# Pooled attention feeding a feed-forward network: the q tiles of batches 1 to 7 transposed by VectorE in 32 by 32 blocks

## The chip, the cores and the metric

The kernel runs on one core of one Trainium2 chip. The metric is the device time of one execution in microseconds (us); less is better. The inputs lie in HBM, and the output is written there.

## The reference

The input is q, k and v of 8 batches, 8 heads, 576 positions and 64 dimensions, and two weight matrices of 512 x 2048 and 2048 x 512, all float32. Cut to what matters:

```python
k_p = k.reshape(B, H, Sp, 8, D).mean(axis=3)      # 576 positions pooled to 72
v_p = v.reshape(B, H, Sp, 8, D).mean(axis=3)
scores = (1 / sqrt(D)) * q @ k_p.transpose(0, 1, 3, 2)
scores = scores - max(scores, axis=-1)
attn = exp(scores)
attn = attn / (sum(attn, axis=-1) + 1e-9)
attn_out = attn @ v_p                             # (8, 8, 576, 64)
x = attn_out.transpose(0, 2, 1, 3).reshape(4608, 512)
h = x @ w_in
return maximum(0.01 * h, h) @ w_out               # (4608, 512)
```

## The kernel before

**The feed-forward part** is most of the work. The 4608 rows of x are taken in nine pieces of 512 (c = 0 to 8), and the 2048 hidden columns in sixteen strips of 128 (f). Each matrix is held as a rounded high part and the remainder, and each product is made of three matmuls (high by high, low by high, high by low). `m1` (L661 to L663) makes a strip of h in PSUM (`ph`), ScalarE applies the leaky step to it (L666) and rounds it to `gh` (L669), and VectorE takes the remainder `gl` (L670). `m2` (L685 to L687) multiplies that with w_out into four accumulators (`acc`), which `store` copies out (L707 and L708) and sends to HBM. The runs are: c = 0 with the first eight strips, c = 1 with all, c = 0 with the rest (the first half comes back from HBM as `partial`), then c = 2 to 8.

**The weights** arrive as bits (`w_bits`, L161 and L165) and are split on the chip into the high and low parts by `convert`: four ScalarE and VectorE operations in `head` (L183 to L189), two in `tail` (L193 and L194). This goes on during the first 160 us, beside the attention of batches 0 and 1.

**The attention** of a batch is split into units, by tiles of 128 or 64 positions; each batch has four tiles of 128 and one of 64, named q1_0 to q1_4 for batch 1. `load_q` fetches a tile with one DMA, positions on the partitions, all 8 heads by 64 dimensions in a row of 512. `q_unit` (L364) has TensorE transpose it in four blocks of 128 columns into a PSUM bank, `pq` (L368), and ScalarE copies that to `qT` (L370), which then holds two heads by 64 dimensions on the partitions. `s_unit` multiplies qT with the pooled keys (`pss`, L393), VectorE takes the maximum of each row (`red`, L401) and ScalarE the exponentials (`e`, L403). `norm_unit` divides by the sum (L414 and L415 on VectorE, `at` on GpSimd, L417 and L421). `p_unit` transposes the result on TensorE (`pp`, L442) and splits it (`pT_hi`, `pT_lo`, `pT_rem`, L444 to L452). `av_unit` multiplies with the pooled values (`pa`, L467 to L470) and writes x, split in two parts (L484 and L485), transposed as `m1` needs it.

**Buffers.** q tiles of batch 0 lie in places that x takes later; those of all other batches share two buffers (`two`, tag `q`), and their qT share two others. The `pq` bank comes from `bank`; for batches 1 to 7 that is one of two PSUM banks, which `pss`, `pp`, `pa`, `pk` and `pv` use too.

**What sets the order.** TensorE's order is written out by hand: the string FIRST for batch 0, and behind it the loop over `beats`, which puts attention units between the matmuls of `m1` and `m2`; `line_up` arranges the units. `qu` asks for the tile two further on as soon as a tile's `q_unit` is issued. The order on the other engines is found by a scheduler that looks at dependences and estimated times. Nearly all DMAs are issued by SyncE (SP), in one queue, in order. Its DMAs take eight completion counters in turn, and each waits for the DMA that is eight before it.

Of the kernel before, what the change touches and what calls it, by code (L numbers as in the profile page):

```python
# [10 lines left out]
F32 = mybir.dt.float32  # L11
# [13 lines left out]
def tile_pooled_attention_ffn(  # L25
# [9 lines left out]
    nc = tc.nc  # L35

    P = 128
# [6 lines left out]
    NK = DM // P  # L44
# [31 lines left out]
    two = ctx.enter_context(tc.tile_pool(name="two", bufs=2))  # L76
# [30 lines left out]
    for g in range(2):  # L107
        r = slice(32 * g, 32 * g + 32)
# [97 lines left out]
    def bank(b, name):  # L206
        nonlocal turn
        pool, tag = banks[turn % len(banks)] if b == 0 else banks[0]
        turn += 1
        return pool.tile([P, NK, P], F32, tag=tag, name=name)  # L210
# [104 lines left out]
    def load_q(b, t):  # L315
        s0, n = tiles[b][t]
        if b == 0:
            qr = one.tile([P, H, D], F32, tag=f"xh1_{t}" if t < NK else "xl1_0", name=f"q{b}_{t}")
        else:
            qr = two.tile([P, H, D], F32, tag="q", name=f"q{b}_{t}")  # L320
        nc.sync.dma_start(qr[:n], q[b, :, s0 : s0 + n, :].rearrange("h s d -> s h d"))
        return qr

    def place_k(b, sums, rem):
# [38 lines left out]

    def q_unit(b, t, qr):  # L364
        n = tiles[b][t][1]
        pq = bank(b, f"pq{b}_{t}")
        for p in range(NK):
            nc.tensor.transpose(pq[:, p, :n], qr[:n, 2 * p : 2 * p + 2, :], ident[:n, :n])  # L368
        qT = two.tile([P, NK, P], F32, tag="qT", name=f"qT{b}_{t}")
        nc.scalar.copy(qT[:, :, :n], pq[:, :, :n])  # L370
        return qT
# [142 lines left out]
    def attention(b):  # L514
# [5 lines left out]
        def loads():  # L520
            (start_k, st["k"]), (start_v, st["v"]) = load_k(b), load_v(b)
            start_k()
            q_of[b, 0] = load_q(b, 0)
            q_of[b, 1] = load_q(b, 1)
            start_v()
            for t in range(2, 5):
                q_of[b, t] = load_q(b, t)
# [18 lines left out]
        def qu(t):  # L546
            def f():
                st["qT", t] = q_unit(b, t, q_of[b, t])
                after = every.index((b, t)) + 2
                if after < len(every) and every[after] not in q_of:  # L550
                    q_of[every[after]] = load_q(*every[after])
            return f
# [210 lines left out]
    for b in range(2, B):  # L763
        for j, piece in enumerate(PIECES[b]):
            c = 2 + (2 * TAIL + S * (b - 2) + piece[0][0]) // CH
# [85 lines left out]
```

## Time and profile before

| what | value |
|---|---|
| three runs | 1004.41, 1009.0 and 1011.04 us; median 1009.0 |
| profiled execution, its own time | 1006.54 us |
| its span in the profile | 1004.8 us |
| mean granted TensorE clock | 0.982 |
| HBM read and written | 46.14 MB and 10.49 MB |
| DMA packets under 512 B | 39856 of 65006 |

PE is TensorE, DVE VectorE, ACT ScalarE, POOL GpSimd and SP SyncE. A row of the timeline gives the start in us, the duration in us, the engine, the line of the code, the operation with output and inputs, and in brackets the idle time before it and what ended it. "x4" in a row means four instructions in one. In the rows that group a whole stretch, the numbers behind the bar are busy us, mean ns of one, and idle us before them with what ended it. Matmuls are pipelined, so the durations of neighbours overlap; their starts tell the pace. The profiled execution is the one whose rows are used for durations.

### The profile page before, as it was taken

How to read it: one execution, taken by the hardware profiler on the slowest of the kernel's cores; microseconds unless marked ns; L12 is line 12 of the kernel's file. 1: busy time of each engine (PE TensorE's matmuls, PEld its weight loads, DVE VectorE, ACT ScalarE, POOL GpSimd, SP SyncE). 2: the span in 40 equal slices, each digit the busy share in tenths (PEclk: the TensorE clock that was granted, in tenths of full speed). 3: DMA queues.
4: the chain of work that ended last, by engine and by line, in shares of the span. 5: the costliest groups of instructions: out<-in, count | busy, mean ns of one | idle time of the engine just before them, and what ended most of it. 6: DMA issues, size and time to landing. Idle time of an engine off the chain costs nothing.

```text
span 1004.8 us, 12738 instructions
## 1 busy us (share of the span) xinstructions
PE 952.5 (95%) x4536; PEld 778.1 (77%) x4536; DVE 371.5 (37%) x902; ACT 428.2 (43%) x1386; POOL 177.4 (18%) x292
## 2 busy tenths in 40 slices
PE   4468899999999999999999999999999999999998
PEld 3457678888787778888887888788877888788886
DVE  5998639323432322233232333233223322221111
ACT  4677766234433343434343434344443433322221
POOL 3602200401116610132013301220110100100000
PEclk9689999999999999999999999999999999999999
DMA  9955311312033400121022202110100010001001
GB/s 241 267 171 149 88 60 42 103 34 69 1 104 101 105 11 17 58 74 32 6 64 58 58 1 69 46 29 1 58 22 11 1 48 1 1 1 42 0 1 42
DMA packets 65006, 57.44 MB, mean 57 GB/s; under 512 B 39856, under 2 KB 48048, under 8 KB 64944
## 3 DMA queue, kind: packets, MB, share of 16 engines
q1 hardware_dynamic: 64944, 56.64, 19.8%
q8 instruction: 36, 0.59, 0.3%
q14 instruction: 26, 0.21, 0.1%
HBM read 46.14 MB, written 10.49 MB: 56 GB/s over the span
## 4 chain that ended last, share of the span: by engine, by line
PE 88%; DVE 5%; ACT 4%; issue 1%; DMA 1%; SPq 1%; POOL 0%; DVEq 0%; ACTq 0%; POOLq 0%
PE ph L661 13%; PE acc L685 13%; PE ph L663 13%; PE ph L662 13%; PE acc L687 13%; PE acc L686 13%; PE pss L393 4%; PE pp L442 3%; PE pq L368 1%; ACT e L403 1%; PE pa L468 1%; PE pa L467 1%; PE pa L470 1%; PE pa L469 1%; SPq L240 1%
## 5 line engine op out<-in xcount | busy, mean ns | idle before, releaser
L661 PE MATMUL ph<-xh,w 128*128 128x512 f32 x576 | 235.8, 409 | 0.0
L685 PE MATMUL acc<-w,gh 128*128 128x512 f32 x576 | 233.7, 406 | 0.0
L663 PE MATMUL ph<-xh,w 128*128 128x512 f32 x576 | 226.3, 393 | 0.0
L662 PE MATMUL ph<-xl,w 128*128 128x512 f32 x576 | 226.1, 393 | 0.0
L687 PE MATMUL acc<-w,gl 128*128 128x512 f32 x576 | 225.7, 392 | 0.0
L686 PE MATMUL acc<-w,gh 128*128 128x512 f32 x576 | 225.5, 392 | 0.0
L670 DVE TENSOR_TENSOR gl<-ph,gh 128x512 fp32r<-128x512 f32 x144 | 99.4, 690 | 263.2 <-ACT gh L669 262.3
L666 ACT ACTIVATE ph<-ph 128x512 f32<-128x512 f32 x144 | 84.2, 585 | 250.4 <-PE ph L663 250.3
L403 ACT ACTIVATE e<-pss,red 128x72 f32<-128x72 f32 (+1 forms) x320 | 98.2, 320 | 115.5 <-DVE red L401 115.3
L417 POOL TENSOR_TENSOR at<-e,red 128x256 f32<-128x256 f32 (+1 forms) x76 | 47.4, 624 | 543.7 <-DVE red L415 267.8
L663 PEld LDWEIGHTS ph<-xh,w 128*128 128x128 f32 x576 | 108.7, 189 | 24.0
L687 PEld LDWEIGHTS acc<-w,gl 128*128 128x128 f32 x576 | 108.4, 188 | 23.8
L685 PEld LDWEIGHTS acc<-w,gh 128*128 128x128 f32 x576 | 108.5, 188 | 22.3 <-issue 1.6
L661 PEld LDWEIGHTS ph<-xh,w 128*128 128x128 f32 x576 | 108.8, 189 | 21.9 <-issue 1.4
L686 PEld LDWEIGHTS acc<-w,gh 128*128 128x128 f32 x576 | 108.7, 189 | 19.7
L662 PEld LDWEIGHTS ph<-xl,w 128*128 128x128 f32 x576 | 108.9, 189 | 19.1
L669 ACT CAST gh<-ph 128x512 fp32r<-128x512 f32 x144 | 85.4, 593 | 3.1
L401 DVE TENSOR_REDUCE red<-pss 128x4 f32<-128x288 f32 (+1 forms) x80 | 36.1, 453 | 94.3 <-PE pss L393 93.2
L403 ACT ACTIVATION_READ_ACCUMULATOR e<-pss,red 128x1 f32 (+1 forms) x320 | 65.4, 204 | 0.0
L393 PEld LDWEIGHTS pss<-kT,qT 128*128 128x128 f32 (+1 forms) x320 | 47.1, 183 | 14.4 <-ACT qT L370 4.9
L393 PE MATMUL pss<-kT,qT 128*128 128x144 f32 (+1 forms) x320 | 53.8, 295 | 4.1 <-ACT qT L370 4.1
L448 DVE TENSOR_TENSOR pT_lo<-pp,pT_hi 128x256 fp32r<-128x256 f32 (+1 forms) x80 | 31.7, 396 | 66.0 <-ACT pT_rem L445 65.3
(93 smaller groups left out, 844.1 us busy)
## 6 DMA issues: line engine op xcount, KB each, us to landing
out_dram<-o SPq DMA_DIRECT2D x35, 256.0 KB, 2.9
q<-in_q_dram SPq DMA_DIRECT2D x32, 256.0 KB, 3.9
w_bits<-in_moe_w_in_dram SPq DMA_DIRECT2D x16, 512.0 KB, 3.7
w_bits<-in_moe_w_out_dram SPq DMA_DIRECT2D x16, 512.0 KB, 3.5
k0raw<-in_k_dram SPq DMA_DIRECT2D x16, 256.0 KB, 3.7
k1raw<-in_k_dram SPq DMA_DIRECT2D x16, 256.0 KB, 4.4
v0raw<-in_v_dram SPq DMA_DIRECT2D x16, 256.0 KB, 3.8
v1raw<-in_v_dram SPq DMA_DIRECT2D x16, 256.0 KB, 5.6
```

What stands on the lines that cost most here:

```text
L393: nc.tensor.matmul(sc[:n, 2 * SP * i : 2 * SP * (i + 1)], qT[:, p, :n], kT[:, p, :, :].rearrange("d i s -> d (i s)"), start=True, stop=True,)
L403: ins = nc.scalar.activation(e[:n, h, :], scv[:n, h, :], AF.Exp, bias=mx[:n, h : h + 1], accum_out=sm[:n, h : h + 1],)
L417: eng.tensor_tensor(at[:n, 0:2, :].rearrange("a i (h s) -> a (i h) s", h=2), e[:n, :, 0:MAIN], sm[:n].unsqueeze(2).broadcast_to([n, 4, MAI ...
L661: nc.tensor.matmul(ph, w[:, 0, ks], xh[kk], start=kk == 0, stop=False)
L662: nc.tensor.matmul(ph, w[:, 0, ks], xl[kk], start=False, stop=False)
L663: nc.tensor.matmul(ph, w[:, 1, ks], xh[kk], start=False, stop=kk == NK - 1)
L666: nc.scalar.activation(ph, ph, AF.Prelu, alpha=0.01)
L669: casts.append(nc.scalar.copy(gh, ph))
L670: nc.vector.tensor_tensor(gl, ph, gh.bitcast(F32), op=ALU.subtract)
L685: nc.tensor.matmul(a, gh[:, r], hi, start=first, stop=False)
L686: nc.tensor.matmul(a, gh[:, r], lo, start=False, stop=False)
L687: nc.tensor.matmul(a, gl[:, r], hi, start=False, stop=last)
```

## The change

For batch 0 nothing changes. For the others a q tile is no longer loaded by one DMA with positions on the partitions. Its 512 columns are four pairs of heads (p) by two heads of a pair (i) by two halves of 32 dimensions (c); its positions are blocks (g) of 32. Sixteen DMAs, one for each i, c and p, put the blocks into the partitions that their columns will have after the transpose: block row 2i + c holds the 32 columns c of head i. Each DMA writes 32 partitions, and moves runs of 32 numbers (128 bytes) where the one DMA moved runs of 64 (256 bytes). VectorE then transposes every block of 32 by 32 in its place, with one instruction for the tile, from the q buffer into qT. The four transposes on TensorE, the PSUM bank and ScalarE's copy of these tiles go: 28 tiles of 128 positions and 7 of 64.

```diff
@@ load_q
-        nc.sync.dma_start(qr[:n], q[b, :, s0 : s0 + n, :].rearrange("h s d -> s h d"))
+        if b == 0:
+            nc.sync.dma_start(qr[:n], q[b, :, s0 : s0 + n, :].rearrange("h s d -> s h d"))
+            return qr
+
+        blocks = qr.rearrange("a h d -> a (h d)").rearrange("a (p g d) -> a p g d", p=NK, d=32)
+        src = q[b, :, s0 : s0 + n, :].rearrange("(p i) (g s) (c d) -> i c s p g d", i=2, s=32, c=2)
+        for i in range(2):
+            for c in range(2):
+                r = 32 * (2 * i + c)
+                for p in range(NK):
+                    nc.sync.dma_start(blocks[r : r + 32, p, : n // 32, :], src[i, c, :, p])
         return qr
@@ q_unit
         n = tiles[b][t][1]
+        if b > 0:
+
+            qT = two.tile([P, NK, P], F32, tag="qT", name=f"qT{b}_{t}")
+            blocks = qr.rearrange("a h d -> a (h d)").rearrange("a (p s) -> a p s", p=NK)
+            nc.vector.transpose(qT[:, :, :n], blocks[:, :, :n])
+            return qT
```

In the changed kernel the lines behind the first insertion are 10 further down, and those behind the second 16: the new DMA is L331, the new transpose L380, L401 becomes L417, and L661 becomes L677.

The order moves at three places. The first is SP's queue about 34 us from the start, where the first two tiles of batch 1 are loaded between strips of weights (`w0_bits4` is strip 4 of w_in, `w1_bits4` of w_out). Before:

```order
L161 DMA w0_bits3_182<-in_moe_w_in_dram 128x4x256
L165 DMA w1_bits3_184<-in_moe_w_out_dram 128x1024
L321 DMA q1_0_365<-in_q_dram 128x8x64
L321 DMA q1_1_566<-in_q_dram 128x8x64
L161 DMA w0_bits4_461<-in_moe_w_in_dram 128x4x256
L165 DMA w1_bits4_463<-in_moe_w_out_dram 128x1024
L161 DMA w0_bits15_1631<-in_moe_w_in_dram 128x4x256
L161 DMA w0_bits5_555<-in_moe_w_in_dram 128x4x256
```

And now:

```order
L161 DMA w0_bits3_182<-in_moe_w_in_dram 128x4x256
L165 DMA w1_bits3_184<-in_moe_w_out_dram 128x1024
L331 DMA q1_0_365<-in_q_dram 32x4x32 x16
L161 DMA w0_bits4_476<-in_moe_w_in_dram 128x4x256
L165 DMA w1_bits4_478<-in_moe_w_out_dram 128x1024
L331 DMA q1_1_581<-in_q_dram 32x4x32 x14
L161 DMA w0_bits5_570<-in_moe_w_in_dram 128x4x256
L331 DMA q1_1_581<-in_q_dram 32x4x32 x2
L161 DMA w0_bits15_1711<-in_moe_w_in_dram 128x4x256
```

Two issues have become 32, and strip 4 and one DMA of strip 5 stand between the pieces of q1_1 and the rest. Further on, q1_4, q2_0 and q2_1 follow each other in SP's queue with one or two weight DMAs between them, sixteen pieces each.

The second place is DVE's list at about 53 us, in the conversion of strip 2 (`w0_t2`, `w1_t2`) and the last score unit of batch 0 (`red0_4`). Before:

```order
L189 ISA w0_t2_519<-w0_bits2_178,w0_t2_519 128x1024
L485 TENSOR_TENSOR xl0_3_409<-pa0_1_3_546,xh0_3_405 128x256
L186 SCALAR_TENSOR_TENSOR w1_t2_569<-w1_bits2_180,w1_t2_569 128x512
L401 TENSOR_REDUCE red0_4_0_581<-pss0_4_0_577 64x4
L401 TENSOR_REDUCE red0_4_1_591<-pss0_4_1_587 64x4
L194 TENSOR_TENSOR w0_2_518<-w0_t2_519,w0_2_518 128x512
L189 ISA w1_t2_569<-w1_bits2_180,w1_t2_569 128x1024
L414 TENSOR_SCALAR red0_4_0_581<-red0_4_0_581 64x4
```

And now:

```order
L189 ISA w0_t2_534<-w0_bits2_178,w0_t2_534 128x1024
L380 STREAM_TRANSPOSE qT1_0_771<-q1_0_365 128x512
L501 TENSOR_TENSOR xl0_3_424<-pa0_1_3_561,xh0_3_420 128x256
L186 SCALAR_TENSOR_TENSOR w1_t2_599<-w1_bits2_180,w1_t2_599 128x512
L417 TENSOR_REDUCE red0_4_0_611<-pss0_4_0_607 64x4
L417 TENSOR_REDUCE red0_4_1_621<-pss0_4_1_617 64x4
L380 STREAM_TRANSPOSE qT1_1_838<-q1_1_581 128x512
L194 TENSOR_TENSOR w0_2_533<-w0_t2_534,w0_2_533 128x512
L189 ISA w1_t2_599<-w1_bits2_180,w1_t2_599 128x1024
L430 TENSOR_SCALAR red0_4_0_611<-red0_4_0_611 64x4
```

The transposes of q1_0 and q1_1 stand among work that was there before; L194, L189 and the normalisation of batch 0's last tile come behind the second of them. Later transposes stand behind the maximum of the second score unit of the tile two before, which frees the qT buffer: q1_2 behind `red1_0_1`, q1_4 behind `red1_2_1`, q2_1 behind `red1_4_1`.

The third place is TensorE's list in the steady part, at about 228 us, around the first tile of batch 2. Before:

```order
L685 MATMUL acc1_3_1534<-w1_14_1761,gh1_14_2022 128x512
L686 MATMUL acc1_3_1534<-w1_14_1761,gh1_14_2022 128x512
L687 MATMUL acc1_3_1534<-w1_14_1761,gl1_14_2023 128x512
L368 MATMUL pq2_0_2129<-ident_87,q2_0_1100 128x128 x4
L661 MATMUL ph0_9_2138<-xh0_0_402,w0_9_1386 128x512
L662 MATMUL ph0_9_2138<-xl0_0_406,w0_9_1386 128x512
L663 MATMUL ph0_9_2138<-xh0_0_402,w0_9_1386 128x512
```

And now:

```order
L701 MATMUL acc1_3_1614<-w1_14_1841,gh1_14_2102 128x512
L702 MATMUL acc1_3_1614<-w1_14_1841,gh1_14_2102 128x512
L703 MATMUL acc1_3_1614<-w1_14_1841,gl1_14_2103 128x512
L677 MATMUL ph0_9_2228<-xh0_0_417,w0_9_1466 128x512
L678 MATMUL ph0_9_2228<-xl0_0_421,w0_9_1466 128x512
L679 MATMUL ph0_9_2228<-xh0_0_417,w0_9_1466 128x512
```

The four transposes are gone, and the rest of TensorE's list is as it was.

## The prediction

> **What bounds the kernel now.** I read the busy shares and the chain of waits first, then the busy time by stage.
>
> ```profile
> span 1004.8 us, 12738 instructions
> PE 952.5 (95%) x4536; PEld 778.1 (77%) x4536; DVE 371.5 (37%) x902; ACT 428.2 (43%) x1386; POOL 177.4 (18%) x292
> PE 88%; DVE 5%; ACT 4%; issue 1%; DMA 1%; SPq 1%; POOL 0%; DVEq 0%; ACTq 0%; POOLq 0%
> ...
> 0.00:58.00 58.00, 27.82 (x134) 22.98 (x134) 45.75 (x115) 34.45 (x136) 25.33 (x42) 0.79 0.93 249
> 58.00:75.00 17.00, 12.21 (x52) 9.44 (x53) 15.57 (x36) 15.03 (x32) 1.48 (x2) 0.80 0.48 152
> 75.00:150.00 75.00, 67.27 (x332) 53.90 (x331) 46.46 (x115) 51.67 (x169) 11.37 (x20) 0.98 0.33 100
> 150.00:900.00 750.00, 745.14 (x3580) 609.11 (x3579) 247.85 (x612) 303.50 (x1008) 139.24 (x228) 1.00 0.15 41
> ```
>
> The stage rows give, after the stretch, the busy us of PE, weight load, DVE, ACT and POOL, then the granted clock, the DMA share and GB/s. From 150 us on PE works 745.14 of 750 us: what leaves PE's list there shortens the run by its own length. Up to 75 us DVE and ACT are the full ones (15.57 and 15.03 of 17 us), and PE waits for them. So the change must be costed twice: as PE time after 150 us, and as DVE and SP work before.
>
> **PE, after 150 us: the gain.** Each removed tile is four transposes between matmuls that run back to back. One tile of 128 rows and one of 64:
>
> ```profile
> 227.43 0.40 PE L686 MATMUL acc<-w,gh 128*128 128x512 f32 x1
> 227.66 0.39 PE L687 MATMUL acc<-w,gl 128*128 128x512 f32 x1
> 227.89 0.60 PE L368 MATMUL pq<-ident,q 128*128 128x128 f32 x4
> 228.24 0.48 PE L661 MATMUL ph<-xh,w 128*128 128x512 f32 x1
> 228.56 0.40 PE L662 MATMUL ph<-xl,w 128*128 128x512 f32 x1
> ...
> 289.14 0.39 PE L663 MATMUL ph<-xh,w 128*128 128x512 f32 x1
> 289.46 0.46 PE L368 MATMUL pq<-ident,q 64*128 64x64 f32 x4
> 289.85 0.50 PE L685 MATMUL acc<-w,gh 128*128 128x512 f32 x1
> 290.18 0.39 PE L686 MATMUL acc<-w,gh 128*128 128x512 f32 x1
> ...
> L368 PE MATMUL pq<-ident,q 128*128 128x128 f32 x96 | 14.4, 272 | 0.0
> L368 PE MATMUL pq<-ident,q 64*128 64x64 f32 x24 | 2.7, 235 | 0.0
> ```
>
> Starts count here, since the durations overlap. A plain step is 227.66 − 227.43 = 0.23 us. From L687 at 227.66 to the second matmul behind the transposes (228.56) it is 0.90 us, where two steps would take 0.46: the tile costs 0.44. The small one costs 290.18 − 289.14 − 0.46 = 0.58. The last two rows, of the stretch from 150 us on, count 96/4 = 24 large and 24/4 = 6 small tiles: 24 × 0.44 + 6 × 0.58 = **14.0 us** gone. The score matmuls behind read qT, which DVE now makes about a tile earlier; with a third of DVE busy there (247.85 of 750) and ACT rid of a copy, nothing new should end last in this stage. Without that cover (qT late by a DVE operation) it would be up to 30 × 0.7 = 21 us.
>
> **PE, before 150 us.** Five q1 tiles go, 4 × 0.44 + 0.58 = 2.3 us. Part of that time PE waits for others anyway, so I count 1 us (bounds 0 and 2.3).
>
> **DVE: the transposes.** The trace of before holds none. Nearest are one-pass DVE rows of the same 128x512 shape, and the ACT copy that goes:
>
> ```profile
> L185 DVE TENSOR_SCALAR w_t<-w_bits 128x512 int32<-128x512 int32 x32 | 13.9, 439 | 1.6 <-DMA partial<-o 1.3 <-ACT w_bits L183 0.2
> L194 DVE TENSOR_TENSOR w<-w_t,w 128x512 fp32r<-128x512 f32 x32 | 24.1, 763 | 2.6 <-ACT w L193 2.5
> L370 ACT COPY qT<-pq 128x512 f32<-128x512 f32 x32 | 19.1, 595 | 27.8 <-PE pq L368 27.7
> ```
>
> So between 0.44 and 0.76 us; I take 0.6, the middle, as no row says which is nearer. Two of them (q1_0, q1_1) stand where DVE is full, near 54 us: **+1.2** (0.9 to 1.5). The others stand where DVE is about 60% busy (46.46 of 75) or less, and cost nothing unless their data is late. [...]
>
> **SP: sixteen issues for one.** This is the term that can eat the gain. What SP spends on an issue:
>
> ```profile
> L321 SPq DMA_DIRECT2D q<-in_q_dram x33: 367/390/616, 74.2 to 817.2; - x33
> DMA to landing us min/median/max: 2.9/3.8/3.9
> ...
> L240 SPq DMA_DIRECT2D k0raw<-in_k_dram x16: 596/602/737, 0.7 to 559.4; - x16
> L165 SPq DMA_DIRECT2D w_bits<-in_moe_w_out_dram x16: 327/341/547, 16.0 to 164.9; - x16
> ```
>
> An issue over 128 partitions takes 0.34 to 0.39 us (L165, L321), one over 64 takes 0.60 (L240, and the 0.616 of L321 is a tile of 64 rows). Fewer partitions are dearer, and 32 are in no row. I take t = 0.65 us a piece: the nearest row and 0.05 between issues. Below, eight completion counters in turn and about 3.6 us to landing allow no less than 3.6/8 = 0.45; above, as much again as from 128 to 64 gives 0.85 and the same ratio 1.0.
>
> In the steady stage 16 × 0.65 = 10.4 us a tile fall into 850/30 = 28 us. The start is where they matter, since DVE works in order and now stands still until all sixteen pieces of a tile have landed:
>
> ```profile
> L321 SPq DMA_DIRECT2D q<-in_q_dram x2: 368/1994/3620, 34.3 to 35.4; - x2
> DMA to landing us min/median/max: 8.7/8.7/8.7
> q<-in_q_dram SPq DMA_DIRECT2D x32, 256.0 KB, 3.9
> ...
> 54.43 0.80 DVE L401 TENSOR_REDUCE red<-pss 64x4 f32<-64x288 f32 x2
> 55.16 0.67 DVE L194 TENSOR_TENSOR w<-w_t,w 128x512 fp32r<-128x512 f32 x1
> 55.76 0.67 DVE L189 CUSTOM_DVE_ANT_0 w_t<-w_bits,w_t 128x1024 uint16<-128x1024 uint16 x1
> 56.55 0.17 DVE L415 RECIPROCAL red<-red 64x4 f32<-64x4 f32 x1
> 57.44 0.41 DVE L414 TENSOR_SCALAR red<-red 64x4 f32<-64x4 f32 x1 [0.72 <-ACT e L403]
> ...
> 56.86 0.61 POOL L417 TENSOR_TENSOR at<-e,red 64x256 f32<-64x256 f32 x1 [13.10 <-DVE red L415]
> 57.52 0.67 PE L442 MATMUL pp<-ident,at 64*128 64x64 f32 x3 [2.85 <-POOL at L417]
> ```
>
> The transpose of q1_1 comes behind the two maxima at 54.43, so at 55.2 + 0.6 (q1_0's) = 55.8. Its pieces: before, q1_1 was issued at 35.4 and landed 8.7 us later, at 44.1, the last of two tiles of q (2 × 256 KB, 2.1 us at the 249 GB/s of that stage), so all that was older had landed at 42. The eighth piece of q1_0 can go then, at the latest. Behind it SP has eight pieces of q1_0, the pair of w4 (0.9), fourteen pieces of q1_1, one weight DMA (0.4), and two pieces: 42 + 24t + 1.3 + 3.6 to land = 62.5 at t = 0.65. DVE stands from 55.8 to 62.5, less the 0.7 us that it idled there anyway: X = 24t − 9.6 = **6 us** (1.2 at t = 0.45, 14.4 at 1.0). Behind the waiting transpose are L194, L189 and the reciprocal L415; POOL's at (13.10 idle) and PE's pp (2.85 idle) wait for that one, so the stall reaches PE in full. [...]
>
> What is late next: from about 82 us, when the transpose of q1_2 (behind the max at 81.00) frees its buffer, SP has the pieces of q1_4, q2_0 and q2_1, 48 issues nearly in a row.
>
> ```profile
> 81.00 0.44 DVE L401 TENSOR_REDUCE red<-pss 128x4 f32<-128x288 f32 x1
> 106.37 0.46 DVE L401 TENSOR_REDUCE red<-pss 128x4 f32<-128x288 f32 x1 [1.54 <-PE pss L393]
> 121.92 0.45 DVE L401 TENSOR_REDUCE red<-pss 64x4 f32<-64x288 f32 x1 [0.32 <-POOL at L421]
> 123.71 0.37 PE pp L442 x3
> ```
>
> q2_1 is transposed behind the max at 121.92 (122.9 with one transpose more ahead), and its buffer comes free at 107.3, behind the max at 106.37. It is in time while 107.3 + 16t + 3.6 < 122.9, t < 0.75; with the queue, Y = 82 + 48t + 1.7 + 3.6 − 122.9 = 48t − 35.6 beyond that. PE's pp at 123.71 follows at once, so Y would reach the end too. At 0.65 it is nothing.
>
> **The sum:** −14.0 − 1 + 1.2 + 6 = −7.8 us. On the profiled execution, whose span is 1004.8 and whose time 1006.5, that is 998.7. The three runs shown have a median of 1009.0, 2.5 above it; the four times together average 1007.8, so I forecast **1000.0**, a gain of 0.8%. One per cent is about what a measurement of this kernel can tell from no change.
>
> **The rivals.** (a) Small pieces are issued fast, t about 0.45: X is 1, and the time 1007.8 − 14.0 − 1 + 1.2 + 1 = 995. For it: a piece moves 16 KB where the L240 row moves 128; against it: the 64-row q tile, half the bytes of the large one, has the longer issue. [...]
>
> (b) Slower: an issue over 32 partitions continues the trend, t = 1.0. Then X = 14.4 and Y = 12.4, and the time is 1007.8 − 13.8 + 26.8 = 1021. The place is SP's queue alone; it takes the whole gain back from t = 0.82 (X + Y = 13.8) and is slower by 1% from about 0.95. For it: 0.34 to 0.60 for half the partitions; against it: 64 partitions take 0.60 whatever they move, which looks like a flat price.
>
> (c) No gain to speak of: t near 0.8, or transposes that also come late at the boundaries between runs, a few us in sum: 1007.8 − 13.8 + 9 + 4 = 1007. For it: the 48 issues leave q2_1 only 1.6 us of slack; against it: 28 us per tile later on.
>
> **How the numbers follow.** Forecast 0.42 (own range 996 to 1004), (a) 0.30 (991 to 998), (c) 0.15 (1004 to 1013), (b) 0.13 (1013 to 1045). Faster by over 1% (under 997.7) is nearly all of (a) and a quarter of the forecast, 0.28 + 0.11 = 0.39; slower by over 1% (above 1017.9) most of (b) and an odd stall, 0.13; the rest, 0.48, within 1%. The range 990 to 1014 leaves out most of (b) and little else.
>
> **What would show it.** The 96 + 24 pq rows behind 150 us are gone, and PE stays full from there to the end, in a stage about 14 us shorter. The STREAM_TRANSPOSE of 128x512 takes 0.44 to 0.76 us. SP's issue of a piece takes near 0.60 us. DVE idles some 6 us ahead of its second transpose, near 56 us, released by the DMA of q, and not ahead of the seventh. The forecast is wrong if issues are far from 0.65, if DVE's wait at 56 us is absent, or if score matmuls wait for qT in the steady stage.

## The result, and the profile after

The changed kernel takes 996.95 us (median of 7 runs, 995.31 to 1000.37), the one before 1005.45 us beside it (7 runs): a ratio of 0.9905, 95% interval 0.9885 to 0.9924. On another chip it was 0.9917 (0.9902 to 0.9932). The forecast was 1000.0, a gain of 0.8%. One execution of the kernel before took 2418 us, on the chip where that kernel's median is 1010.52; it is left out of the ratios.

The profile after, first its head, then the same stages as before (the columns are again PE, weight load, DVE, ACT and POOL busy, granted clock, DMA share, GB/s):

```profile
span 995.2 us, 13059 instructions
PE 938.7 (94%) x4396; PEld 768.8 (77%) x4396; DVE 387.7 (39%) x937; ACT 411.5 (41%) x1351; POOL 179.1 (18%) x292
```

```profile
0.00:58.00 58.00, 29.05 (x131) 24.43 (x131) 43.56 (x110) 34.94 (x136) 25.07 (x40) 0.79 0.81 208
58.00:75.00 17.00, 9.76 (x36) 7.88 (x37) 12.59 (x29) 9.13 (x20) 3.27 (x4) 0.60 0.70 212
75.00:150.00 75.00, 65.16 (x315) 51.75 (x314) 53.04 (x129) 52.46 (x171) 11.33 (x20) 0.98 0.40 115
150.00:900.00 750.00, 744.23 (x3518) 610.07 (x3517) 264.29 (x647) 293.46 (x986) 139.44 (x228) 1.00 0.17 41
```

PE has 140 matmuls fewer (4396 for 4536), and is as full as before from 150 us on (744.23 of 750). The loss stands in the second row: DVE 12.59 busy of 17 us, where it was 15.57, and ACT 9.13 for 15.03. DVE's timeline shows why:

```profile
52.63 0.71 DVE L380 STREAM_TRANSPOSE qT<-q 128x512 f32<-128x512 f32 x1
53.25 0.40 DVE L501 TENSOR_TENSOR xl<-pa,xh 128x256 fp32r<-128x256 f32 x1
53.56 0.68 DVE L186 SCALAR_TENSOR_TENSOR w_t<-w_bits,w_t 128x512 int32<-128x512 int32 x1
54.16 0.82 DVE L417 TENSOR_REDUCE red<-pss 64x4 f32<-64x288 f32 x2
59.88 0.71 DVE L380 STREAM_TRANSPOSE qT<-q 128x512 f32<-128x512 f32 x1 [4.90 <-DMA q<-in_q_dram]
60.51 0.65 DVE L194 TENSOR_TENSOR w<-w_t,w 128x512 fp32r<-128x512 f32 x1
```

The transpose of q1_1 waits 4.90 us for its pieces. What is behind it reaches POOL and PE late; PE's pp started at 57.52 before, with 2.85 us of idle time ahead of it, and now starts at 63.14, with 9.22:

```profile
63.14 0.47 PE L458 MATMUL pp<-ident,at 64*128 64x64 f32 x2 [9.22 <-POOL at L433]
```

In the steady part the place at which the four transposes stood is a plain step of 0.23 us (230.65 to 230.88):

```profile
230.42 0.39 PE L702 MATMUL acc<-w,gh 128*128 128x512 f32 x1
230.65 0.40 PE L703 MATMUL acc<-w,gl 128*128 128x512 f32 x1
230.88 0.39 PE L677 MATMUL ph<-xh,w 128*128 128x512 f32 x1
231.12 0.39 PE L678 MATMUL ph<-xl,w 128*128 128x512 f32 x1
```

**A ruler for all that follows.** PE's list is written by hand, and without the transposes of q (which are left out of the count where they differ) it is the same in all kernels here, matmul for matmul. So the start of the n-th matmul in one trace minus its start in another says how far the one has fallen behind. The table gives that difference against the kernel before, at five places of that kernel's time, and at the end (us). Each row is one profiled execution, which need not be a typical one: that of "q1_0 and q1_1 as before" was the shortest of five, 2.8 us under their median, and those of the last two rows were the longest of their kernels, 5.4 and 2.6 us over.

```
                                        57.5    75   110   150    500    end
changed kernel                          +5.6  +4.2  +4.4  +3.0   -1.0   -9.5
changed kernel, again                   +5.7  +4.2  +7.7  +6.3   +2.0   -6.5
batch 1 as before                       -0.5  -0.3  +0.2  +1.7   -2.1  -10.6
two transposes queued later             -0.9  -1.7  -1.0  -2.4   -7.1  -15.6
two transposes queued later, again      -0.3  -2.1  -1.3  -2.8   -7.1  -15.5
q1_0 and q1_1 as before                 -1.1  +0.5  -2.1  -3.6   -9.6  -18.1
transposes done twice                   +5.3  +3.7  +7.3  +6.3   +1.8   -6.6
batch 1 alone changed                   +4.8  +4.1  +7.9  +6.3   +5.8   +5.8
transposes left in on PE                +5.0  +4.5  +8.3  +6.9  +17.2  +21.9
PE transposes of a constant             +7.1  +6.5 +10.4  +8.7   +9.9   +9.9
32 pieces a tile                        +5.5  +5.1  +5.7  +9.0   +7.7   -0.7
```

For the changed kernel it reads: 5.6 behind at 57.5 us, 3.0 to 6.3 behind at 150, and from there 12.5 to 12.8 won back. Two sides, as the prediction had them: a loss at the start, a gain behind it.

### The profile page after: what moved, and what is told of

Same layout as the page of the kernel before. It is cut to its first block, busy times and chain, and to the rows that moved or that the text cites. A ratio compares the mean times of both kernels' runs of the same rounds, so it can differ in the third digit from the quotient of the medians.

```text
span 995.2 us, 13059 instructions
## 1 busy us (share of the span) xinstructions
PE 938.7 (94%) x4396; PEld 768.8 (77%) x4396; DVE 387.7 (39%) x937; ACT 411.5 (41%) x1351; POOL 179.1 (18%) x292
## 2 busy tenths in 40 slices
DMA packets 105667, 57.50 MB, mean 58 GB/s; under 512 B 80512, under 2 KB 88704, under 8 KB 105600
## 3 DMA queue, kind: packets, MB, share of 16 engines
q1 hardware_dynamic: 105600, 56.67, 21.7%
## 4 chain that ended last, share of the span: by engine, by line
PE 86%; DMA 5%; ACT 3%; SPq 3%; DVE 2%; issue 1%; POOL 0%; DVEq 0%; ACTq 0%
PE ph L677 13%; PE acc L701 13%; PE ph L679 13%; PE ph L678 13%; PE acc L703 13%; PE acc L702 13%; PE pss L409 3%; PE pp L458 2%; DMA q<-in_q_dram 2%; DMA w_bits<-in_moe_w_in_dram 1%; DMA v0raw<-in_v_dram 1%; SPq L331 1%; PE pa L483 1%; PE pa L484 1%; SPq L240 1%
## 5 line engine op out<-in xcount | busy, mean ns | idle before, releaser
L677 PE MATMUL ph<-xh,w 128*128 128x512 f32 x576 | 235.1, 408 | 0.0
L677 PEld LDWEIGHTS ph<-xh,w 128*128 128x128 f32 x576 | 109.1, 189 | 22.2 <-issue 1.4
L417 DVE TENSOR_REDUCE red<-pss 128x4 f32<-128x288 f32 (+1 forms) x80 | 36.1, 453 | 83.8 <-PE pss L409 83.0
L409 PE MATMUL pss<-kT,qT 128*128 128x144 f32 (+1 forms) x320 | 55.8, 303 | 8.4 <-ACT qT L386 4.0
L458 PE MATMUL pp<-ident,at 128*128 128x128 f32 (+1 forms) x240 | 40.6, 282 | 19.4 <-POOL at L433 9.2
```

The costliest lines, as they stand in the source:

```text
L409: nc.tensor.matmul(sc[:n, 2 * SP * i : 2 * SP * (i + 1)], qT[:, p, :n], kT[:, p, :, :].rearrange("d i s -> d (i s)"), start=True, stop=True,)
L458: nc.tensor.transpose(pp[:, i, :n], at[:n, i, :], ident[:n, :n])
L677: nc.tensor.matmul(ph, w[:, 0, ks], xh[kk], start=kk == 0, stop=False)
```

## The experiments

### Where the start loses: batch 1 as before

The edit sends batch 1 the old way:

```diff
-        if b == 0:
+        if b < 2:
             nc.sync.dma_start(qr[:n], q[b, :, s0 : s0 + n, :].rearrange("h s d -> s h d"))
...
-        if b > 0:
+        if b > 1:
```

> Batch 1 is loaded and transposed as before (one DMA a tile, TensorE, ScalarE's copy); only batches 2 to 7 have the blocks and VectorE's transpose. Theory 'stall': the changed kernel reaches 150 us 3.0 us later than the one before because VectorE stands 4.9 us ahead of q1_1's transpose at 55 us. Then the start is that of before (offset of TensorE's list at 150 us within 1 us of 0), 12 to 12.5 us are won after it, and the time is about 993 to 994, 3 to 4 below the changed kernel. Rival 'absorbed': the stall is made good later and the 3.0 us come from q2_0, q2_1 and the general load of SP: the time is that of the changed kernel, 997, or up to 2.3 us more for the five tiles that are back on TensorE.

Measured: 995.17 us beside 1010.52 of the kernel before on that chip, ratio 0.9858 (0.9829 to 0.9886), some 5 us under the changed kernel by the ratios, 2 to 4 by the medians. (On that chip the kernel before lies at 1005.5 to 1006.7 us in five executions and at 1010.5 to 1011.5 in five others, which makes the interval wide.) By the table PE is within 0.5 us of the kernel before up to 110 us. The 1.7 at 150, where 1 was expected at most, is new at about 115 us: matmuls follow each other there by 0.43 us instead of 0.23, and from 113 to 117 us the granted clock is 0.57 in this trace and 1.00 before. So the loss at 57.5 us belongs to batch 1, and it is not made good later: theory "stall".

### The stall alone: two transposes queued later

Here everything is as in the changed kernel, loads too; only the order on DVE differs.

```diff
-        nc.vector.reciprocal(sm[:n], sm[:n])
+        rec = nc.vector.reciprocal(sm[:n], sm[:n])
+        if b == 0:
+            anchor["rec"] = rec
...
-            nc.vector.transpose(qT[:, :, :n], blocks[:, :, :n])
+            with tc.issue_after(anchor["rec"].ins) if b == 1 and t < 2 else nullcontext():
+                nc.vector.transpose(qT[:, :, :n], blocks[:, :, :n])
```

> Everything as in the changed kernel, but the transposes of q1_0 and q1_1 are queued on VectorE behind the normalisation of batch 0's last tile (four small operations further on), so that nothing that TensorE wait for at 57 us stands behind them. Theory 'stall': TensorE's pp, 63.1 us in the changed kernel, is back at 57 to 58; VectorE still waits some 2 to 3 us for the pieces, with the conversion of strip 3 behind; the time falls by 2 to 5, to 992 to 995. Rival 'VectorE is full anyway': what is not lost ahead of pp is lost in the conversion of the weights behind it; less than 1 us, 996 to 998.

Measured: 992.11 us beside 1010.52, ratio 0.9832 (0.9807 to 0.9858). DVE's and PE's timeline of this kernel:

```profile
55.68 0.17 DVE L432 RECIPROCAL red<-red 64x4 f32<-64x4 f32 x1
56.58 0.41 DVE L431 TENSOR_SCALAR red<-red 64x4 f32<-64x4 f32 x1 [0.72 <-ACT e L420]
57.02 0.17 DVE L432 RECIPROCAL red<-red 64x4 f32<-64x4 f32 x1
57.39 0.71 DVE L381 STREAM_TRANSPOSE qT<-q 128x512 f32<-128x512 f32 x1 [0.20 <-DMA w_bits<-in_moe_w_in_dram]
58.75 0.71 DVE L381 STREAM_TRANSPOSE qT<-q 128x512 f32<-128x512 f32 x1 [0.64 <-DMA q<-in_q_dram]
```

```profile
56.66 0.63 PE L461 MATMUL pp<-ident,at 64*128 64x64 f32 x3 [1.11 <-POOL at L436]
57.22 0.50 PE L680 MATMUL ph<-xh,w 128*128 128x512 f32 x1
```

The work that POOL and PE wait for now passes ahead of the transposes, and these find their data almost there: 0.64 us of waiting for 4.90. PE's pp starts at 56.66 instead of 63.14, and the start is 2.4 us ahead of the kernel before, where the changed kernel is 3.0 to 6.3 behind. The gain is larger than the 2 to 5 us that were expected, and DVE's wait shorter than the 2 to 3. The rival, that DVE would lose behind the place what it wins ahead of it, falls. Run once more on another chip, this version gave the same:

> The two transposes behind the normalisation of batch 0's last tile, once more on another chip and beside the kernels of this call: the ratio to the kernel before is 0.983 within 0.004, 7 us or more under the changed kernel's.

Measured: 991.03 us beside 1008.48, ratio 0.9834 (0.9816 to 0.9853). It beats both kernels, the changed one by some 7 to 8 us by the ratios. The two were not timed on one chip, but the run with transposes done twice (below), which takes as long as the changed kernel, was: 1000.23 us beside 992.11.

### Only the two tiles

The edit keeps the old way for b = 0 and for the first two tiles of batch 1:

```diff
-        if b == 0:
+        if b == 0 or b == 1 and t < 2:
...
-        if b > 0:
+        if b > 1 or b == 1 and t > 1:
```

> Only q1_0 and q1_1 are loaded and transposed as before (their 32 pieces leave SP's queue at 34 to 57 us, their transposes VectorE's), the other 33 tiles as in the changed kernel. Theory 'those two tiles carry the loss': TensorE's list is within 1 us of before up to 75 us, and the ratio is about that of the two transposes queued later, 0.983 to 0.986. Rival 'the later tiles of batch 1 and q2_0, q2_1 cost as much in the start': the first 150 us stay 2 to 3 us longer than before, and the ratio is 0.988 to 0.991.

Measured: 991.15 us, ratio 0.9837 (0.9818 to 0.9855), PE 1.1 us ahead at 57.5, 0.5 behind at 75 and 3.6 ahead at 150. So q1_0 and q1_1 carry the loss, and the five tiles behind them show none. The two repairs are worth the same, though the second leaves two tiles on PE and takes 32 pieces from SP's queue.

### Batch 1 alone

Only batch 1 has the pieces and the DVE transpose; the tests read `b != 1` and `b == 1`.

> Only batch 1 has the sixteen pieces and VectorE's transpose; all other batches are as before. Theory 'the start loses': the first 150 us take 1 to 3 us longer than before although 2.3 us of TensorE work are gone, and nothing is won behind them, so the time is 1 to 3 us above the kernel before (ratio 1.001 to 1.003). Rival: batch 1 gains its 2.3 us like the others: ratio 0.998.

Measured: 1010.57 us beside 1006.77, ratio 1.0034 (1.0021 to 1.0048): a loss of 3.4 us, a little more than was expected, although PE has 2.3 us less to do. In the start, the first of the two places at which it acts, the change by itself loses.

### Is the gain PE's time? Transposes left in

The four PE transposes of each tile of batches 2 to 7 are put back into a bank that nobody reads; loads, DVE's transposes and the missing ACT copy stay as changed.

```diff
             nc.vector.transpose(qT[:, :, :n], blocks[:, :, :n])
+            if b > 1:
+                pq = bank(b, f"pq{b}_{t}")
+                for p in range(NK):
+                    nc.tensor.transpose(pq[:, p, :n], qr[:n, 2 * p : 2 * p + 2, :], ident[:n, :n])
             return qT
```

> The changed kernel, with the four TensorE transposes of each tile of batches 2 to 7 put back into a PSUM bank that nobody reads; loads, VectorE's transposes and the missing copies on ScalarE as in the changed kernel. Theory 'TensorE time': the whole gain after 150 us is the time of these instructions, so 24 x 0.44 + 6 x 0.58 = 14 us come back, less what a matmul neighbour hides: 1009 to 1011, above the kernel before by the 3 us of the start. Rival 'waits': part of the gain was waiting for ScalarE's copy qT or for the bank; then only some 5 to 9 us come back, 1002 to 1006.

Measured: 1026.84 us, ratio 1.0172 (1.014 to 1.0204), more than either theory had. Beside an even growth there are jumps of 7.8, 3.3 and 1.3 us, near 300, 509 and 818 us of the changed kernel's time. PE's waits from 150 us on, then SP's timeline at the first of them:

```profile
PE acc L705 <- DVE o L725: 7.7, 1, 7.7
PE acc L705 <- DVE o L728: 4.2, 2, 3.1
```

```profile
254.97 44.33 SPq L331 DMA_DIRECT2D q<-in_q_dram  x32
299.65 1.27 SPq L240 DMA_DIRECT2D k0raw<-in_k_dram  x2
300.96 4.87 SPq L331 DMA_DIRECT2D q<-in_q_dram  x10
307.45 1.26 SPq L240 DMA_DIRECT2D k1raw<-in_k_dram  x2
308.75 1.54 SPq L331 DMA_DIRECT2D q<-in_q_dram  x3
310.34 1.40 SPq L732 DMA_DIRECT2D out_dram<-o  x3
```

```profile
289.82 0.60 PE L384 MATMUL pq<-ident,q 128*128 128x128 f32 x4
296.35 0.46 PE L384 MATMUL pq<-ident,q 64*128 64x64 f32 x4
```

The kernel held each q buffer until PE had read it (the last two rows: q2_3 and q2_4), so the pieces of the tiles that take these buffers stood at the head of SP's queue until then, and the stores of o behind them left at 310.34 (the changed kernel's first one at 292.35). The accumulators were freed late, and PE waited. This run mixes two things, PE's time and q buffers that are held longer. In the next one the transposes read a constant:

```diff
+                    nc.tensor.transpose(pq[:, p, :n], ident[:n, :], ident[:n, :n])
```

> As the run that left TensorE's transposes in, but they read the constant identity instead of the q tile, so that the q buffer is free as soon as VectorE has transposed it. The result nobody reads. Theory 'TensorE time': 24 x 0.44 + 6 x 0.58 = 14 us more than the changed kernel, spread evenly over the 30 tiles of batches 2 to 7, and no single wait over 2 us at the ends of the runs. If the waits of 7.8 and 3.3 us of that other run (TensorE for VectorE's copies o, behind SP's stores) remain, they came from the bank or from TensorE, not from the q buffer that was held longer, and the time is 1020 or more.

Measured: 1010.89 us, ratio 1.0044 (1.0024 to 1.0063), beside 0.9917 of the changed kernel on the same chip, so 12.8 us more. The waits are gone (none of PE on o from 150 us on). Against the changed kernel's trace on that chip, the difference grows from 2.4 us at 150 to 16.4 at the end: 14.0 us, spread evenly. The count of these instructions:

```profile
L384 PE MATMUL pq<-ident 128*128 128x128 f32 x96 | 14.4, 272 | 0.0
L384 PE MATMUL pq<-ident 64*128 64x64 f32 x24 | 2.7, 235 | 0.0
```

That is the predicted 24 x 0.44 + 6 x 0.58 = 14.0, though the agreement to a tenth is chance: the ratios give 12.8 us and the medians 11.6. Read from one matmul ahead of each place to five behind it, the places themselves are 0.47 us longer (24 of them) and 0.61 (six), 14.9 in all, and the rest of the list differs by 1 us the other way. The gain behind 150 us is PE's list growing shorter; within about 2 us nothing else is left to explain.

The changed kernel on the same chip, for comparison:

> The changed kernel once more, on the chip of the runs beside it, so that they can be compared without the difference between chips: the ratio to the kernel before is 0.9905 within 0.003.

Measured: 999.33 us beside 1006.77, ratio 0.9917 (0.9902 to 0.9932).

### Is DVE in the way? Transposes twice

```diff
-            nc.vector.transpose(qT[:, :, :n], blocks[:, :, :n])
+            for _ in range(2 if b > 1 else 1):
+                nc.vector.transpose(qT[:, :, :n], blocks[:, :, :n])
```

> Each tile of batches 2 to 7 is transposed twice in a row by VectorE, the second time over the first; 30 more operations of 0.4 to 0.7 us, about 19 us of VectorE. Theory 'hidden': VectorE is a third busy after 150 us and qT is made about a tile ahead of its use, so the time moves by less than 1 us: 996 to 998. Rival 'in the way': the transposes stand ahead of operations that TensorE waits for (gl, pT_lo, xl), so half or all of the 19 us show: 1006 to 1016.

Measured: 1000.23 us, ratio 0.9918 (0.9889 to 0.9948), the changed kernel's within the intervals. The table has 12.9 us won from 150 us to the end, for 12.5 and 12.8. Thirty more DVE operations, about 19 us, cost nothing that can be measured, which the interval puts at no more than some 3 us (the 996 to 998 us that were expected hold for another chip). The cover that the prediction named is there, for two transposes as for one.

### What the pieces cost SP: 32 and 64 a tile

Each piece of batches 2 to 7 is cut in two, or into its blocks of 32 positions, m being 2 or 1 for a large tile.

```diff
-                    nc.sync.dma_start(blocks[r : r + 32, p, : n // 32, :], src[i, c, :, p])
+                    for g in range(0, n // 32, m):
+                        nc.sync.dma_start(blocks[r : r + 32, p, g : g + m, :], src[i, c, :, p, g : g + m])
```

> Each piece of batches 2 to 7 is cut in two: 32 DMAs a tile. At 0.475 us each, SP needs 15.2 us a tile, with tiles every 28 us on average but closer within a run. Theory 'a price per issue, and stores stand behind the pieces': some runs' ends have TensorE wait for VectorE's copies o, for which the stores of o are late; 5 to 40 us more than the changed kernel. Rival 'half full is free': within 2 us of the changed kernel, ratio 0.990.

Measured with 32: 1003.01 us, ratio 0.9948 (0.9932 to 0.9964), 3 to 4 us above the changed kernel by the ratios: between the 5 that the theory had at least and the 2 that the rival had at most. In the traces 7.0 us are lost at once, between 152 and 156 us of the changed kernel's first trace, where a run ends: 4.0 in the wait below, and the rest behind it, where matmuls follow each other by 0.43 us instead of 0.23.

```profile
PE acc L703 <- DVE o L726: 4.0, 1, 4.0
```

```profile
139.84 16.23 SPq L333 DMA_DIRECT2D q<-in_q_dram  x28
156.17 0.37 SPq L728 DMA_DIRECT2D partial<-o  x1
156.59 1.37 SPq L333 DMA_DIRECT2D q<-in_q_dram  x3
158.06 1.40 SPq L728 DMA_DIRECT2D partial<-o  x3
```

The stores of `partial` stand behind 28 pieces and leave at 156 to 159 us, where the changed kernel's left at 148 to 152. Behind that place nothing more is lost: the run is 8.8 us behind that trace there and 8.7 at the end.

> Each piece of batches 2 to 7 is cut into four (one block of 32 positions each, 4 KB): 64 DMAs a tile instead of 16. Theory 'a price per issue': each still takes SP about 0.475 us, so a tile takes 30 us of SP, and tiles come every 28 us: SP falls behind, transposes and the stores behind them in SP's queue come late, and the time is 1030 to 1100. Rival 'a price per byte': 4 KB are issued in a quarter of the time, and the time stays within 3 us of the changed kernel.

Measured with 64, in a single execution: 1222.78 us, more than the 1100 of the theory. The chain of waits goes over to SP, and PE's longest waits are for the copies o:

```profile
SPq 46%; PE 32%; DMA 9%; issue 6%; POOL 4%; DVE 2%; ACT 2%; POOLq 0%; DVEq 0%; ACTq 0%
```

```profile
508.71 31.06 SPq L333 DMA_DIRECT2D q<-in_q_dram  x64
```

```profile
PE acc L703 <- DVE o L726: 159.3, 6, 44.0
PE acc L703 <- DVE o L723: 35.5, 1, 35.5
```

A piece of 4 KB takes 31.06/64 = 0.485 us, one of 16 KB 0.475: between these two sizes the price is per issue, not per byte. The theory had the price right and the damage too small, because it counted late transposes (7.0 us of PE's waiting) and not the stores of o: they stand behind tiles of 31 us in one queue, and PE waited 195 us for the accumulators.

## Why the prediction was right

**Direction and size.** Forecast -7.8 us, measured -8.5 by the medians and -0.83% to -0.95% by the ratios. Both sides of the sum came out: the gain behind 150 us as its one term, the loss before it as a sum of terms of which some were off against each other. The time alone does not choose between the forecast and rival (a): 996.95 lies in the ranges of both.

**PE after 150 us: -14.0.** Right. The thirty places are 14.9 us shorter in the traces of the changed kernel too, and 12.5 to 12.8 arrive at the end. No score matmul waits for qT there. What is lost again in the first trace is mostly one stretch: at 324.77 `pa` starts 0.8 us late, since it now waits 0.64 us for an ACT operation that stands in another order, and from 331 to 335 us the granted clock is 0.60, where it was 1.00 before: matmuls follow each other there by 0.43 us instead of 0.23, and PE falls another 1.6 us behind (1.0 at 329.58, 2.6 at 335.93). The run with q1_0 and q1_1 as before has neither, and 14.5 us arrive there.

**The start: +6.2 forecast (-1 + 1.2 + 6), +3.0 and +6.3 in the two traces.** The place, the waiting instruction, what is queued behind it and who waits were as described. At the place PE fell 5.6 us behind (63.14 for 57.52), where the two terms 1.2 and 6 make 7.2. The -1 for PE's shorter list can't be read beside the stall; with the stall taken away the start is 2.4 to 3.6 us ahead of the kernel before, so the term was too small. That is more than the 2.3 us of the five tiles' transposes; where the rest comes from was not traced. The size of the stall was 4.9 for 6, but by other numbers than the working had. The issue price, its central one, was wrong, and by the prediction's own sign (issues far from 0.65) this step failed:

```profile
42.53 4.11 SPq L331 DMA_DIRECT2D q<-in_q_dram  x9
46.77 0.39 SPq L161 DMA_DIRECT2D w_bits<-in_moe_w_in_dram  x1
47.26 0.44 SPq L165 DMA_DIRECT2D w_bits<-in_moe_w_out_dram  x1
47.75 7.42 SPq L331 DMA_DIRECT2D q<-in_q_dram  x14
55.27 0.39 SPq L161 DMA_DIRECT2D w_bits<-in_moe_w_in_dram  x1
55.70 0.98 SPq L331 DMA_DIRECT2D q<-in_q_dram  x2
...
L331 SPq DMA_DIRECT2D q<-in_q_dram x560: 311/430/1750, 33.8 to 779.9; - x187
```

A piece takes 0.43 us and 0.045 to the next: t = 0.475, not 0.65. The trend from 128 to 64 partitions, which rival (b) carried on, does not go on to 32, and neither does the flat 0.60 that the forecast took. It is the price of rival (a), whose formula gives X = 24 x 0.475 - 9.6 = 1.8. What made it 4.9: the queue was free of older transfers at 42.9 rather than 42.0 and one piece of the fourteen waited a microsecond for its counter, going out at 52.01 when the DMA of w_out eight ahead of it (issued at 47.26) had landed at 51.99 (together the last landing at 59.9 where the formula has 58.3, 1.6 us); the transpose was due at 55.0 rather than 55.8; and the 0.7 us of idle time that was taken off belongs to the operations behind it. 1.8 + 1.6 + 0.8 + 0.7 = 4.9. So the forecast's X was near by luck: a price that was too high by 24 x 0.175 = 4.2 us, and 3.1 us that were not counted. Rival (a) failed on the rest of the formula, not on the price.

**The transposes.** Forecast 0.6 us within 0.44 to 0.76, measured:

```profile
L380 DVE STREAM_TRANSPOSE qT<-q 128x512 f32<-128x512 f32 x28 | 19.8, 706 | 4.9 <-DMA q<-in_q_dram 4.9
L380 DVE STREAM_TRANSPOSE qT<-q 128x256 f32<-128x256 f32 x7 | 3.1, 438 | 0.0
```

The first row also answers the question of q2_1: 4.9 us, once, is all that any transpose waits for a DMA. At t = 0.475 the later queue (Y, due from t = 0.75) was in time. The step from 256 to 512 elements is 0.268 us, 1.05 ns for each, and by these two rows what lies above that is 0.17 us an instruction. The 0.6 was an estimate, the middle between rows of other operations; the measured 0.71 us lies near the upper end of that range.

**Rivals.** (b) and (c) did not come to pass, but the run with 64 pieces shows (b)'s mechanism, SP's queue as the bound, at its full size, and by a way that the prediction had looked past: the stores in the same queue.

## What to carry to other kernels

Work taken from the engine that hardly ever waits was worth nearly its own time here (12.5 to 12.8 of 14.9 us). Work given to an engine that takes its list in order cost nothing where its data was in time, and a stall where it was late: look at what stands behind the new instruction, and queue the instruction behind that (here 7 to 8 us for putting two transposes behind the six operations that followed them). Many small DMAs are paid for on the queue that issues them, here some 0.48 us each for 4 KB and for 16 KB, and by everything behind them in it. Before cutting a transfer into pieces, multiply their number by the issue time, and look for the stores in the same queue whose buffers someone needs.

## What the runs showed of the hardware

SP's issue time neither falls nor rises steadily with the partitions in these DMAs: 0.34 to 0.39 us for 128 and 0.60 for 64 in the kernel before (the L240 row moves 256 KB an issue, not 128 as the prediction has it; a q tile of 64 rows moves 128 KB and took 0.60 at 306.54), 0.43 for 32 in the changed kernel (0.31 for the piece at 52.01, which had waited for its counter), the last alike for 4 and 16 KB (0.485 and 0.475 us from one issue to the next).

Runs of 128 bytes instead of 256 doubled the packets under 512 B (80512 for 39856), and the hardware queue's share of the 16 DMA engines went from 19.8% to 21.7%. The row of before, then two of after:

```profile
q1 hardware_dynamic: 64944, 56.64, 19.8%
...
DMA packets 105667, 57.50 MB, mean 58 GB/s; under 512 B 80512, under 2 KB 88704, under 8 KB 105600
q1 hardware_dynamic: 105600, 56.67, 21.7%
```

Behind some waits of PE the granted clock was lower. From 58 to 75 us it was 0.60 in the changed kernel, where PE had waited 9.22 us, and 0.80 before, where it had waited 2.85. The length of the wait alone does not decide it: behind the same wait of 2.1 us at 113 us the clock was 1.00 in the kernel before and 0.57 with batch 1 as before. And two executions of the changed kernel, alike within 0.1 us up to 75 us, differ by 3.3 at 110: from 90 to 98 us the one was granted 1.00 and the other 0.79. The two rows, the changed kernel's first trace and the second:

```profile
90.00:98.00 8.00, 8.00 (x44) 6.78 (x43) 7.53 (x18) 6.82 (x28) 3.17 (x6) 1.00 0.12 19
```

```profile
90.00:98.00 8.00, 7.30 (x29) 6.04 (x30) 6.83 (x19) 4.22 (x18) 2.20 (x4) 0.79 0.12 23
```

Whether the clock is the cause of the 3.3 us was not tried; it says that a single trace of this start is good to some 3 us. Three other kernels of the table that share this start (transposes done twice, batch 1 alone, transposes left in) are 7.3 to 8.3 behind at 110, like the second trace. The times show the same: six of the twelve executions of the changed kernel took 995.3 to 997.5 us and six 999.3 to 1000.4, and the two traces are one of each.
